# A list schedule that counts GpSimd's late begin after VectorE, with other durations and a first part of six feature blocks

## The chip, the core and the metric

The kernel runs on one NeuronCore of a Trainium2 chip. Its engines work side by side, each on its own queue of instructions: TensorE (PE in the profile, with PEld for its weight loads), VectorE (DVE), ScalarE (ACT), GpSimd (POOL), and SyncE (SP), which here starts the DMA transfers. The metric is the time of one execution on the device in microseconds; less is better.

## The reference

Banded attention over four batches, eight heads, 768 positions and a head size of 64, and behind it a feed-forward layer over the 3072 tokens (width 512, inner width 2048) whose activation is `h * cos(h)`:

```python
scores = scale * np.matmul(q, k.transpose(0, 1, 3, 2))
keep = is_global | is_local          # 8 global columns, a band of 96 behind each row
scores = np.where(keep, scores + bias, -1000000000.0)
a = np.exp(scores - np.max(scores, axis=-1, keepdims=True))
out = np.matmul(a / (np.sum(a, axis=-1, keepdims=True) + 1e-09), v)
x = out.transpose(0, 2, 1, 3).reshape(B * S, H * D)
h = x @ w_in                         # 3072 x 512 by 512 x 2048
result = (h * np.cos(h)) @ w_out     # by 2048 x 512
```

## The kernel before

The 3072 tokens are cut into eight chunks of 384. A chunk's attention is four units of two heads each, so there are 32 units. A unit is loaded, its scores are formed on TensorE (L534 for the first eight units, L538 for the others), the band is folded and the smallest value of a row taken on VectorE (L551, L560), exponentials with their sums come from ScalarE (L585), the rows are normalised (L608, L613, on VectorE or GpSimd), turned by TensorE (L675), masked on VectorE (L683, L688), multiplied with v (L710), and the result is split into a rounded part `xh` (L260 or L262) and a rest `xl` (L731).

The feed-forward layer goes by steps. One step is one chunk and one block of 128 of the 2048 features: its first product is 12 matmuls of 384 columns (L746), then come the turns (L763), the angle (L766), the cosine (L769), the product with h (L804), the split into `gh` (L260, L262 or L264) and `gl` (L813), and the second product, 9 matmuls of 512 columns (L757), some steps later. There are 8 chunks times 16 blocks, 128 steps. In what follows, step 0 is the first one, and a step's first and second product are meant by that number.

The two weight matrices come from HBM in 16 tiles each, as 64-bit words. Each of the 32 tiles is made into two float parts by six operations: `wlow` (L384, L386), `wsign` (L391, L394), `wbias` (L400, L402), `wjoin` (L405, VectorE alone), `whigh` (L260, L262, L264) and `wrest` (L415, VectorE or GpSimd). Once made, a tile stays in SBUF. The order of the steps is the list `PHASES`: chunk 0 with its first eight feature blocks, chunk 1 with all sixteen, chunk 0 with the other eight, then chunks 2 to 7 with all. So the first steps need few weight tiles and one chunk of attention.

The order on every queue is made on the host before the kernel is built, by a list scheduler (class `Plan`). Each operation has the engines that may do it with a duration in ns for each, what it comes after, the buffers it uses and a due time. Going forward in time, each free engine takes the ready operation that is due first, where another engine would not do it for less, counted with the factors `WEIGHT`. VectorE and GpSimd share a way into SBUF; the scheduler keeps those of VectorE's operations that are marked `port` and all of GpSimd's apart, and `emit` makes a GpSimd instruction wait for the marked VectorE instruction that stands before it in the plan. Where the plan leaves TensorE a gap, `emit` fills it with matmuls on zeros (L1054), up to `FILL_TO` in the plan's time.

Of the kernel before, what the change touches and what calls it, by code (L numbers as in the profile page):

```python
# [40 lines left out]
PE, ACT, DVE, POOL, SP = "PE", "ACT", "DVE", "POOL", "SP"  # L41
# [2 lines left out]
PERIOD = 5200  # L44
LAG = 3.5
MARGIN, EACH = 3.2, 3.2
EARLY = {0: 3000, 1: 6000}
WEIGHT = {PE: 1, ACT: 0.5, DVE: 1.2, POOL: 0.8}

PHASES = [(0, 0, 8), (1, 0, 16), (0, 8, 16)]  # L50

PIECES = {-1: [(0, 128), (128, 384)]}
NT, NST, NPV, NX, NV, NRAW, NQK, NRR, NG = 5, 5, 3, 2, 3, 3, 2, 3, 2
# [4 lines left out]

HOMES = 7

FILL_TO, FILL_REST, FILL_EACH, FILL_FIRST, FILL_COLD = 45000, 150, 250, 10, 7000


class Slot:


    def __init__(self, cls, make):
        self.cls, self.make = cls, make
        self.users = 0
        self.at = None  # L70
        self._tile = None
# [19 lines left out]
class Plan:  # L91
# [6 lines left out]
    TABLE = 1300  # L98
    SWITCH = 200

    def __init__(self, places, free):
        self.ops = []
        self.places = {c: list(v) for c, v in places.items()}
        self.busy = {}
        self.free = dict(free)
        self.port = 0
        self.mode = None

    def op(self, engines, emit, after=(), uses=(), due=None, table=None, extra=0, port=False, mode=None):
# [20 lines left out]
    def run(self):  # L130

        self.dues()
        for i, o in enumerate(self.ops):
            o.key = (o.due - min(o.engines.values()), i)
        ready = {e: [] for e in self.free}
        coming = []
        for o in self.ops:
            if o.left == 0:
                for e in o.engines:
                    ready[e].append(o)  # L140
        table = "exp"
        out = []
        dma = 0
        t = 0
        inf = 10**12
        todo = len(self.ops)
        import heapq

        heap = sorted(set(self.free.values()))
        while todo:  # L150
            assert heap, [(o.engines, o.key) for e in ready for o in ready[e]][:20]
            t = heapq.heappop(heap)
            while heap and heap[0] == t:
                heapq.heappop(heap)
            again = True
            while again:
                again = False
                for e, f in self.free.items():
                    if f > t:
                        continue  # L160
                    best = None
                    held = self.port > t
                    holds = lambda o, x: x == POOL or (x == DVE and o.port)
                    for o in ready[e]:
                        if o.ready > t or (best is not None and o.key >= best.key):
                            continue
                        if held and holds(o, e):
                            continue
                        if len(o.engines) > 1:
                            wait = lambda x: max(t, self.free[x], self.port if holds(o, x) else 0) - t  # L170
                            cost = lambda x: wait(x) + o.engines[x] * WEIGHT[x]
                            if any(cost(x) < cost(e) for x in o.engines if x != e):
                                continue
                        taken, ok = set(), True
                        for u in o.uses:
                            if u.at is None:
                                p = next(
                                    (p for p in self.places[u.cls] if self.busy.get(p, 0) <= t and p not in taken),
                                    None,
                                )  # L180
                                if p is None:
                                    ok = False
                                    break
                                taken.add(p)
                        if ok:
                            best = o
                    if best is None:
                        continue
                    o = best
                    if e == ACT and o.table and table and o.table != table:  # L190
                        same = [x for x in ready[e] if x.table == table and x.ready <= t]
                        if table == "exp" and same:
                            o = min(same, key=lambda x: x.key)
                    for u in o.uses:
                        if u.at is None:
                            u.at, u.begin = self.place(u, t), t
                            self.busy[u.at] = inf
                    for x in o.engines:
                        ready[x].remove(o)
                    d = o.engines[e]  # L200
                    if e == ACT and o.table and o.table != table:
                        d += self.TABLE
                        table = o.table
                    if e == PE:
                        if o.mode != self.mode:
                            d += self.SWITCH
                        self.mode = o.mode
                    o.start, o.engine = t, e
                    end = t + d
                    if holds(o, e):  # L210
                        self.port = end
                    self.free[e] = end
                    heapq.heappush(heap, end)
                    if e == SP:
                        dma = max(end + 300, dma) + o.extra

                        self.free[SP] = max(end, dma - DEPTH)
                        heapq.heappush(heap, self.free[SP])
                        end = dma + 1400
                    out.append(o)  # L220
                    todo -= 1
                    for u in o.uses:
                        u.users -= 1
                        u.end = max(getattr(u, "end", 0), end + self.WAIT[e])
                        if u.users == 0:
                            self.busy[u.at] = u.end
                            heapq.heappush(heap, u.end)
                    for n in o.then:
                        n.left -= 1
                        n.ready = max(n.ready, end + (self.WAIT[e] if list(n.engines) != [e] else 0))  # L230
                        if n.left == 0:
                            for x in n.engines:
                                ready[x].append(n)
                            heapq.heappush(heap, max(t, n.ready))
                    again = True
        self.length = max(self.free.values())
        return out


class Net:  # L240
# [123 lines left out]
    def plan_weights(self, f):  # L364


        nc, p = self.nc, self.plan
# [3 lines left out]
        for kind, src, out in (("wi", cols, self.wi), ("wo", rows, self.wo)):  # L371
# [45 lines left out]
                )  # L417

            o = p.op({SP: 470}, dma, extra=1460)
            o = p.op({ACT: 580, DVE: 500, POOL: 700}, wlow, [o], port=True)  # L420
            o = p.op({DVE: 650, POOL: 1310}, wsign, [o], port=True)
            o = p.op({ACT: 580, DVE: 345, POOL: 640}, wbias, [o], port=True)
            o = p.op({DVE: 600}, wjoin, [o], [wu], port=True)
            o = p.op({ACT: 525, DVE: 335, POOL: 595}, whigh, [o], [wu], port=True)
# [49 lines left out]
    def plan_unit(self, L, pr):  # L474
# [4 lines left out]
        nc, p, D = self.nc, self.plan, self.D  # L479
        u = dict(L, pr=pr)  # L480
        n, first = u["n"], u["first"]
# [6 lines left out]
        if exact:  # L488
# [13 lines left out]
            o = p.op({SP: 470}, load, [], [raw], extra=1422 * (QK - k0) // 1000)  # L502
# [7 lines left out]
        st = u["st"] = Slot("st", lambda i: self.work.tile([R, 6 * CT], F32, name="st", tag=i))  # L510
# [8 lines left out]
        ttr = []  # L519
        for js, h in [(js, h) for js in (((0, 1),) if exact else ((0,), (1,))) for h in range(0, CT, 2)]:  # L520
# [25 lines left out]
            for j, ps in pss.items():  # L546
# [6 lines left out]
                o = p.op({DVE: 70 + 98 * (2 - i0)}, fold, [so], [ps])  # L553
# [21 lines left out]
        def worst(e):  # L575
            nc.vector.tensor_tensor(self.worst[:R], self.worst[:R], st.tile[:, :n2], op=ALU.max)

        self.chain("worst", p.op({DVE: 80}, worst, [o for _, o in ttr], [st], due=self.xdue(n, pr), port=True))
        exps = []
        for (t, j), o in ttr:  # L580

# [13 lines left out]
        def rec(e):  # L595
            nc.vector.reciprocal(st.tile[:, 2 * n2 :], st.tile[:, n2 : 2 * n2])

        o = p.op({DVE: 85}, add, exps, [st], port=True)
        o = p.op({DVE: 120}, rec, [o], [st], port=True)
        u["norm"] = []  # L600
        for h in range(0, CT, 2):
# [169 lines left out]
    def plan_step(self, s, n, f, a, b):  # L771

        nc, p = self.nc, self.plan
        due = s * PERIOD
        x = self.x[n]
# [19 lines left out]
        for c0, c1 in pieces:  # L795
            w = c1 - c0
            cs = slice(c0, c1)
            r, h = lambda cs=cs: rr.tile[:, cs], lambda cs=cs: ph.tile[:, cs]
            act, dve, pool = 50 + w * 427 // 512, 70 + w * 535 // 512, 100 + w * 1125 // 512
            o = p.op({ACT: act}, lambda e, r=r, h=h: self.turns(e, r(), h()), [done], [ph, rr])  # L800
            o = p.op({DVE: dve}, lambda e, r=r, h=h: self.angle(e, r(), h()), [o], [ph, rr])
            o = p.op({ACT: act + 135}, lambda e, r=r: self.cosine(e, r()), [o], [rr], table="sin")
# [320 lines left out]
```

## Time and profile before

| what | value |
|---|---|
| median of 3 runs | 706.49 us (705.99 to 707.34) |
| the profiled execution | 704.92 us, its span 703.2 us |
| TensorE busy | 681.4 us (97% of the span) |
| VectorE, ScalarE, GpSimd busy | 506.0, 450.2, 140.1 us |
| granted clock over the span | 0.990 |

A share of the whole span says little here, since the kernel has two stages. In the first some 80 us all engines are at work on weights and on the attention of the first two chunks; after it TensorE hardly ever stands still. The profile is therefore read by stretches of time.

### The profile page before, as it was taken

How to read it: one execution, taken by the hardware profiler on the slowest of the kernel's cores; microseconds unless marked ns; L12 is line 12 of the kernel's file. 1: busy time of each engine (PE TensorE's matmuls, PEld its weight loads, DVE VectorE, ACT ScalarE, POOL GpSimd, SP SyncE). 2: the span in 40 equal slices, each digit the busy share in tenths (PEclk: the TensorE clock that was granted, in tenths of full speed). 3: DMA queues.
4: the chain of work that ended last, by engine and by line, in shares of the span. 5: the costliest groups of instructions: out<-in, count | busy, mean ns of one | idle time of the engine just before them, and what ended most of it. 6: DMA issues, size and time to landing. Idle time of an engine off the chain costs nothing. (4 is left out here: it accounts for less than half of the span.)

```text
span 703.2 us, 12932 instructions
## 1 busy us (share of the span) xinstructions
PE 681.4 (97%) x4448; PEld 595.5 (85%) x4448; DVE 506.0 (72%) x1531; ACT 450.2 (64%) x1129; POOL 140.1 (20%) x180
## 2 busy tenths in 40 slices
PE   8988899999999999999999999999999999999995
PEld 5666799888898888989888898888889888998994
DVE  7998988997847778478776877568784877733442
ACT  6899996776736666467666666476673666634342
POOL 4565665433002121010000121011000112000000
PEclk8999999999999999999999999999999999999998
DMA  9998600013223322032320422212122300001001
GB/s 296 322 305 255 194 22 25 24 46 84 86 67 98 78 60 59 1 104 66 69 68 1 113 62 59 59 57 71 43 68 69 113 27 2 1 1 46 0 1 50
DMA packets 32603, 55.74 MB, mean 79 GB/s; under 512 B 3472, under 2 KB 18192, under 8 KB 32528
## 3 DMA queue, kind: packets, MB, share of 16 engines
q1 hardware_dynamic: 32528, 54.82, 27.1%
q8 instruction: 37, 0.61, 0.4%
q14 instruction: 38, 0.31, 0.1%
HBM read 48.52 MB, written 6.29 MB: 78 GB/s over the span
## 5 line engine op out<-in xcount | busy, mean ns | idle before, releaser
L746 PE MATMUL bank<-xh,w 128*128 128x384 f32 x1024 | 296.7, 343 | 0.6 <-DVE rr L804 0.6
L757 PE MATMUL bank<-w,gh 128*128 128x512 f32 x768 | 245.5, 401 | 0.0
L746 PEld LDWEIGHTS bank<-xh,w 128*128 128x128 f32 x1024 | 188.7, 188 | 8.0 <-DVE rr L804 1.5
L746 PE MATMUL bank<-xl,w 128*128 128x384 f32 x512 | 173.3, 339 | 0.2 <-DVE xl L731 0.2
L757 PEld LDWEIGHTS bank<-w,gh 128*128 128x128 f32 x768 | 138.3, 188 | 22.1 <-issue 0.5
L757 PE MATMUL bank<-w,gl 128*128 128x512 f32 x384 | 151.5, 395 | 0.0
L763 ACT ACTIVATE rr<-bank 128x384 int32<-128x384 f32 x129 | 62.0, 482 | 130.8 <-PE bank L746 128.9
L766 DVE SCALAR_TENSOR_TENSOR rr<-rr,bank 128x384 f32<-128x384 int32 x129 | 69.9, 542 | 103.3 <-ACT rr L763 102.9
L769 ACT ACTIVATE rr<-rr,half_pi 128x384 f32<-128x384 f32 x129 | 78.6, 613 | 40.2 <-DVE rr L766 38.6
L746 PEld LDWEIGHTS bank<-xl,w 128*128 128x128 f32 x512 | 96.7, 189 | 4.3 <-DVE xl L731 0.4
L804 DVE TENSOR_TENSOR rr<-bank,rr 128x384 f32<-128x384 f32 x129 | 70.6, 551 | 37.7 <-ACT rr L769 37.4
L585 ACT ACTIVATE tt<-tt,st 96x104 f32<-96x104 f32 (+1 forms) x256 | 94.3, 370 | 3.9 <-DVE st L560 3.3
L757 PEld LDWEIGHTS bank<-w,gl 128*128 128x128 f32 x384 | 72.1, 188 | 17.3
L813 DVE TENSOR_TENSOR gl<-rr,gh 128x384 fp32r<-128x384 f32 (+1 forms) x114 | 67.9, 595 | 10.2 <-ACT gh L260 7.4
L264 POOL TENSOR_SCALAR ks<-raw 128x408 fp32r<-128x408 f32 (+1 forms) x34 | 19.4, 570 | 273.7 <-PE bank L538 204.7
L260 ACT CAST gh<-rr 128x384 fp32r<-128x384 f32 (+1 forms) x97 | 49.2, 508 | 27.4 <-DVE rr L804 18.8
L560 DVE CUSTOM_DVE_ANT_0 tt<-bank,dd 96x104 f32<-96x104 f32 (+1 forms) x256 | 55.8, 257 | 2.9
L710 PEld LDWEIGHTS bank<-pv,v 104*64 104x64 f32 (+1 forms) x960 | 42.6, 140 | 12.2 <-issue 7.7
L710 PE MATMUL bank<-pv,v 104*64 104x96 f32 (+1 forms) x960 | 49.1, 254 | 1.2 <-ACT pv L260 1.2
L538 PEld LDWEIGHTS bank<-ks,qs 128*96 128x96 f32 x384 | 45.8, 162 | 4.7 <-issue 0.3
L585 ACT ACTIVATION_READ_ACCUMULATOR tt<-tt,st 96x1 f32 x256 | 48.1, 188 | 0.0
L538 PE MATMUL bank<-ks,qs 128*96 128x200 f32 (+1 forms) x384 | 47.9, 254 | 0.0
(95 smaller groups left out, 705.3 us busy)
## 6 DMA issues: line engine op xcount, KB each, us to landing
raw<-in_qk_dram SPq DMA_DIRECT2D x48, 224.0 KB
raw<-in_qk_dram SPq DMA_DIRECT2D x48, 198.0 KB
raw<-in_w_in_dram SPq DMA_DIRECT2D x16, 512.0 KB
raw<-in_w_out_dram SPq DMA_DIRECT2D x16, 512.0 KB
out_dram<-oo SPq DMA_DIRECT2D x24, 256.0 KB
v<-in_v_dram SPq DMA_DIRECT2D x16, 240.0 KB
v<-in_v_dram SPq DMA_DIRECT2D x16, 192.0 KB
raw<-in_qk_dram SPq DMA_DIRECT2D x4, 448.0 KB
```

Of the source, the lines that this page charges most:

```text
L260: self.nc.scalar.copy(out, x)
L538: nc.tensor.matmul(out, qs[:, m, q0], ks[:, k : k + w], start=m == 0, stop=m == 1)
L560: nc.vector.tensor_tensor_reduce(tt[t // 2].tile[:, t % 2, j, :w], ps.tile[:R, i * WIN : i * WIN + w], self.dd[:, v, :w], op0=ALU.add, op1 ...
L585: nc.scalar.activation(x, x, AF.Exp, bias=st.tile[:, c : c + 1], scale=-1.0, accum_out=st.tile[:, n2 + c : n2 + c + 1])
L710: nc.tensor.matmul(px.tile[j * D : (j + 1) * D, t * R : (t + 1) * R], vs.tile[:k, t + c, hs][:, j * D : (j + 1) * D], pv[:k, c, o : o + R] ...
L746: self.nc.tensor.matmul(ph[:, :CW], self.wi[f][:, w, kk * P : (kk + 1) * P], xx[:, kk, :], start=kk == 0 and m == 0, stop=kk == self.NK - ...
L757: self.nc.tensor.matmul(po, gg[:, ts], self.wo[f][:, w, :], start=start and m == 0, stop=stop and m == 2)
L763: self.nc.scalar.activation(r.bitcast(I32), ph, AF.Copy, scale=1.0 / TWO_PI, bias=0.25)
L766: self.nc.vector.scalar_tensor_tensor(r, r.bitcast(I32), -TWO_PI, ph, op0=ALU.mult, op1=ALU.add)
L769: self.nc.scalar.activation(r, r, AF.Sin, bias=self.half_pi)
L804: {DVE: dve}, lambda e, r=r, h=h: nc.vector.tensor_tensor(r(), h(), r(), op=ALU.mult), [o], [ph, rr]
L813: self.eng(e).tensor_tensor(g[1][:, cs], r(), g[0].bitcast(F32)[:, cs], op=ALU.subtract)
```

## The change

The scheduler gets a time `HAND` of 170 ns: GpSimd begins nothing until so long after a marked VectorE operation has ended, and this waiting is counted where an operation's engine is chosen. Some durations are raised: two of GpSimd's weight operations and its `gl` by 40, 40 and 20 ns, and two small ones on VectorE. GpSimd's factor in the choice falls from 0.8 to 0.6, chunk 0's due times are spread by 2000 rather than 3000, chunk 0's first part has six feature blocks rather than eight, and gaps are filled until 100,000 rather than 45,000 ns of the plan. No operation is added to or taken from the computation; all that differs is the order on the queues, which engine does what, and how many filler matmuls there are.

```diff
-EARLY = {0: 3000, 1: 6000}
-WEIGHT = {PE: 1, ACT: 0.5, DVE: 1.2, POOL: 0.8}
-PHASES = [(0, 0, 8), (1, 0, 16), (0, 8, 16)]
+EARLY = {0: 2000, 1: 6000}
+WEIGHT = {PE: 1, ACT: 0.5, DVE: 1.2, POOL: 0.6}
+PHASES = [(0, 0, 6), (1, 0, 16), (0, 6, 16)]
-FILL_TO, FILL_REST, FILL_EACH, FILL_FIRST, FILL_COLD = 45000, 150, 250, 10, 7000
+FILL_TO, FILL_REST, FILL_EACH, FILL_FIRST, FILL_COLD = 100000, 150, 250, 10, 7000
...
+    HAND = 170
...
-                        if held and holds(o, e):
+                        if held and holds(o, e) or e == POOL and self.hand > t:
                             continue
                         if len(o.engines) > 1:
-                            wait = lambda x: max(t, self.free[x], self.port if holds(o, x) else 0) - t
+                            turn = lambda x: (self.hand if x == POOL else 0, self.port if holds(o, x) else 0)
+                            wait = lambda x: max(t, self.free[x], *turn(x)) - t
...
                     if holds(o, e):
                         self.port = end
+                        if e == DVE:
+                            self.hand = end + self.HAND
+                            heapq.heappush(heap, self.hand)
...
-            o = p.op({ACT: 580, DVE: 500, POOL: 700}, wlow, [o], port=True)
-            o = p.op({DVE: 650, POOL: 1310}, wsign, [o], port=True)
+            o = p.op({ACT: 580, DVE: 500, POOL: 740}, wlow, [o], port=True)
+            o = p.op({DVE: 650, POOL: 1350}, wsign, [o], port=True)
...
-        self.chain("worst", p.op({DVE: 80}, worst, [o for _, o in ttr], [st], due=self.xdue(n, pr), port=True))
+        self.chain("worst", p.op({DVE: 100}, worst, [o for _, o in ttr], [st], due=self.xdue(n, pr), port=True))
...
-        o = p.op({DVE: 85}, add, exps, [st], port=True)
+        o = p.op({DVE: 195}, add, exps, [st], port=True)
...
-            act, dve, pool = 50 + w * 427 // 512, 70 + w * 535 // 512, 100 + w * 1125 // 512
+            act, dve, pool = 50 + w * 427 // 512, 70 + w * 535 // 512, 120 + w * 1125 // 512
```

Lines of the kernel after stand up to six further down than before (`wjoin` is L405 before and L411 after). Two places show what moves. The first is VectorE's queue before the normalisation of the eighth unit, whose turning closes the first stage on TensorE; `tt` is a tile of exponentials, `wu` a joined weight tile, `st` the row sums. Before:

```order
L576 TENSOR_TENSOR worst_115<-worst_115,st_806 96x8
L391 TENSOR_SCALAR raw_131<-raw_131 128x512
L415 TENSOR_TENSOR w_1108<-wu_1099,w_1108 128x512
L731 TENSOR_TENSOR xl_853<-bank_1080,xh_852 128x384
L593 TENSOR_SCALAR st_1040<-st_1040 96x8
L596 RECIPROCAL st_1040<-st_1040 96x8
L405 SCALAR_TENSOR_TENSOR wu_1132<-raw_129 128x512
L613 TENSOR_TENSOR tt_1039<-tt_1039,st_1040 96x416
```

After:

```order
L810 TENSOR_TENSOR rr_988<-bank_942,rr_988 128x384
L582 TENSOR_TENSOR worst_115<-worst_115,st_1009 96x8
L411 SCALAR_TENSOR_TENSOR wu_1101<-raw_127 128x512
L819 TENSOR_TENSOR gl_1078<-rr_932,gh_1077 128x384
L411 SCALAR_TENSOR_TENSOR wu_1113<-raw_129 128x512
L599 TENSOR_SCALAR st_1009<-st_1009 96x8
L602 RECIPROCAL st_1009<-st_1009 96x8
L397 TENSOR_SCALAR raw_134<-raw_134 128x512
L619 TENSOR_TENSOR tt_1008<-tt_1008,st_1009 96x416
L619 TENSOR_TENSOR tt_1080<-tt_1080,st_1009 96x416
```

Before, only one half of the unit is normalised here (L613) and the other half is GpSimd's; after, both halves stand here (L619), and the `wrest` that stood in this stretch (L415) has gone.

The second place is GpSimd's queue in the middle of that stage. Before:

```order
L386 TENSOR_SCALAR raw_127<-raw_127 128x512
L402 TENSOR_SCALAR raw_125<-raw_125 128x512
L813 TENSOR_TENSOR gl_785<-rr_703,gh_784 128x384
L394 TENSOR_SCALAR raw_132<-raw_132 128x512
L386 TENSOR_SCALAR raw_134<-raw_134 128x512
L394 TENSOR_SCALAR raw_127<-raw_127 128x512
L394 TENSOR_SCALAR raw_134<-raw_134 128x512
L386 TENSOR_SCALAR raw_136<-raw_136 128x512
L386 TENSOR_SCALAR raw_138<-raw_138 128x512
L415 TENSOR_TENSOR w_970<-wu_959,w_970 128x512
L415 TENSOR_TENSOR w_998<-wu_975,w_998 128x512
L386 TENSOR_SCALAR raw_142<-raw_142 128x512
```

After:

```order
L619 TENSOR_TENSOR tt_621<-tt_621,st_622 96x416
L619 TENSOR_TENSOR tt_729<-tt_729,st_622 96x416
L270 TENSOR_SCALAR gh_812<-rr_679 128x384
L421 TENSOR_TENSOR w_789<-wu_774,w_789 128x512
L819 TENSOR_TENSOR gl_813<-rr_679,gh_812 128x384
L270 TENSOR_SCALAR gh_854<-rr_699 128x384
L400 TENSOR_SCALAR raw_127<-raw_127 128x512
L819 TENSOR_TENSOR gl_855<-rr_699,gh_854 128x384
L408 TENSOR_SCALAR raw_127<-raw_127 128x512
L400 TENSOR_SCALAR raw_129<-raw_129 128x512
L400 TENSOR_SCALAR raw_131<-raw_131 128x512
L421 TENSOR_TENSOR w_978<-wu_964,w_978 128x512
```

Before, the rows are mostly `wlow` and `wsign` (L386, L394); after, `wlow` is gone from here, and two normalisations (L619), three `wrest` (L421), two `gh` (L270) and two `gl` (L819) stand between the `wsign` (L400). Counted over GpSimd's queue up to where the eighth unit is turned, `wlow` goes from 12 to 3, `wrest` from 3 to 7, whole normalisations from 0 to 4 and `gh` from 0 to 3.

## Rows read from the trace of the kernel before

**Rows 1.** Busy time by stretches: us, then each engine's busy us (instructions), clock, DMA share, GB/s.

```profile
20.00:40.00 20.00, 18.34 (x169) 12.50 (x170) 19.93 (x77) 18.48 (x54) 10.86 (x11) 1.00 0.97 283
40.00:60.00 20.00, 16.55 (x115) 13.08 (x115) 18.00 (x60) 18.59 (x53) 11.27 (x12) 0.91 0.86 284
60.00:80.00 20.00, 16.39 (x141) 13.16 (x141) 19.30 (x63) 19.88 (x50) 12.47 (x13) 1.00 1.02 306
100.00:120.00 20.00, 20.00 (x102) 18.15 (x101) 15.01 (x25) 14.47 (x29) 11.61 (x10) 1.00 0.15 41
7.64:78.59 70.95, 59.96 (x501) 45.24 (x497) 66.76 (x265) 64.95 (x197) 39.40 (x42) 0.93 0.97 306
```

**Rows 2.** Timeline of TensorE: start us, us, instructions, [idle before <- releaser].

```profile
48.99 0.51 PE L675 MATMUL bank<-ident,tt 96*104 96x96 f32 x4 [2.13 <-DVE pv L688]
...
52.63 2.12 PE L710 MATMUL bank<-pv,v 104*64 104x96 f32 x32
...
78.59 0.51 PE L675 MATMUL bank<-ident,tt 96*104 96x96 f32 x4 [2.07 <-DVE tt L613]
...
93.79 0.64 PE L757 MATMUL bank<-w,gh 128*128 128x512 f32 x2
```

**Rows 3.** Pieces of the chain that ended last: start us, us, what.

```profile
443.60 1.48 PE bank L710 x32
...
452.31 2.12 PE bank L746 x12
454.43 2.11 PE bank L757 x9
```

**Rows 4.** VectorE by line, 10 to 84 us: busy us, mean ns | idle before, releaser.

```profile
L405 DVE SCALAR_TENSOR_TENSOR wu<-raw 128x512 uint32<-128x512 uint32 x14 | 9.4, 676 | 0.0
L415 DVE TENSOR_TENSOR w<-wu,w 128x512 fp32r<-128x512 f32 x10 | 7.8, 784 | 0.1
L613 DVE TENSOR_TENSOR tt<-tt,st 96x416 f32<-96x416 f32 x11 | 6.9, 649 | 0.0
...
L813 DVE TENSOR_TENSOR gl<-rr,gh 128x384 fp32r<-128x384 f32 x3 | 2.2, 749 | 0.0
...
L391 DVE TENSOR_SCALAR raw<-raw 128x512 uint16<-128x512 uint16 x2 | 1.5, 734 | 0.0
```

**Rows 5.** ScalarE by line, 10 to 84 us.

```profile
L384 ACT ACTIVATE raw<-raw 128x512 int32<-128x512 uint32 x13 | 8.5, 677 | 0.0
L400 ACT ACTIVATE raw<-raw 128x512 f32<-128x512 f32 x10 | 6.8, 683 | 1.3 <-POOL raw L394 1.3
L260 ACT CAST w<-wu 128x512 fp32r<-128x512 f32 x11 | 6.7, 612 | 0.2 <-DVE worst L576 0.2
L769 ACT ACT_TABLE_LOAD x5 | 6.4, 1283 | 0.1
L585 ACT ACT_TABLE_LOAD x4 | 5.1, 1283 | 0.1
...
L260 ACT CAST xh<-bank 128x384 fp32r<-128x384 f32 x7 | 3.3, 467 | 2.1 <-PE bank L710 2.1
```

**Rows 6.** Timeline of ScalarE.

```profile
54.79 0.48 ACT L260 CAST xh<-bank 128x384 fp32r<-128x384 f32 x1 [1.07 <-PE bank L710]
...
87.83 1.14 ACT L260 CAST w<-wu 128x512 fp32r<-128x512 f32 x2
```

**Rows 7.** TensorE's filler matmuls, 0 to 90 us, by line.

```profile
L1054 PE MATMUL idle<-zeros 128*128 128x512 bf16 x30 | 9.4, 464 | 1.1 <-DVE zeros L270 1.1
```

**Rows 8.** GpSimd by line, 10 to 84 us.

```profile
L394 POOL TENSOR_SCALAR raw<-raw 128x512 bf16<-128x512 bf16 x14 | 18.8, 1355 | 15.2 <-DVE wu L405 7.3 <-DVE w L415 4.1 <-DVE st L596 3.0
L386 POOL TENSOR_SCALAR raw<-raw 128x512 int32<-128x512 uint32 x12 | 9.3, 772 | 6.3 <-DVE tt L613 4.5 <-DVE wu L405 1.1
L415 POOL TENSOR_TENSOR w<-wu,w 128x512 fp32r<-128x512 f32 x4 | 5.2, 1288 | 4.9 <-DVE raw L391 2.1 <-ACT rr L763 1.7 <-ACT tt L585 1.1
...
L613 POOL TENSOR_TENSOR tt<-tt,st 96x416 f32<-96x416 f32 x1 | 0.9, 877 | 1.5 <-DVE tt L613 1.5
```

More of the change, by code (lines that the diff above doesn't have):

```diff
@@ L105, in __init__ @@
         self.free = dict(free)
-        self.port = 0
+        self.port = self.hand = 0
         self.mode = None
```

## The prediction

> **What bounds the kernel now.** I read the busy times by stretches first [rows 1]. TensorE is busy for 20.00 of the 20 us from 100 to 120, but for 16.55 and 16.39 of 20 from 40 to 60 and 60 to 80, and filler matmuls are counted as busy there. In those early stretches VectorE is busy for 18.00 to 19.93 of 20 and ScalarE for 18.48 to 19.88. So the kernel has a first stage that VectorE and ScalarE set, and behind it TensorE works without a gap on a load that the change leaves alone: the same matmuls, only in another order. What the change is worth is what it makes of the time that TensorE loses in the first stage.
>
> Where that stage ends is seen in TensorE's timeline [rows 2]: at 78.59 the eighth unit is turned, after 2.07 us of waiting for a normalisation on VectorE. From there on no long gap follows. A microsecond by which this point comes earlier, with the same TensorE work done by then, is a microsecond of the whole.
>
> I need TensorE's own pace to say what "the same work" is. In the chain that ended last [rows 3], a first product takes 2.12 us for 12 matmuls, 0.177 each, a second product 2.11 for 9, 0.234 each, and a unit's product with v 1.48 for 32.
>
> **The change on VectorE.** I counted in both orders what has to be done on each queue before TensorE can turn the eighth unit: everything that stands ahead of the last instruction it needs. On VectorE, after against before: `wjoin` 11 for 13, `wrest` 2 for 9, whole normalisations 7 for 11, one `wsign` and one `gl` fewer. By the means of [rows 4] that is 2 x 0.676 + 7 x 0.784 + 4 x 0.649 + 0.734 + 0.749 = 10.9 us less. One product of the cosine and one small operation more cost at most 0.65 each, the length of a normalisation: I take 9.6 less. Two weight casts fewer and two casts of `xh` more I set equal; all of them are shorter than a normalisation.
>
> TensorE by then has done nine matmuls more of the first products and nine fewer of the second: 9 x 0.177 - 9 x 0.234 = 0.5 us that it owes. If VectorE alone set the point, it would come 9.6 - 0.5 = 9.1 us earlier. That is the upper bound of the gain.
>
> **What is late next: ScalarE.** `wlow`, which GpSimd gives up, goes to ScalarE, and ScalarE had little room. For every first and second product I compared the work that ScalarE must have done with TensorE's own; the difference is largest, after the change, at the second product of step 6. There, after against before, ScalarE has ahead of it six `wlow` and two `wbias` more, one weight cast, two `xh` casts and one scaling of queries fewer, two `gh` fewer for two copies of an output part more, and two table loads fewer, one of each kind. By [rows 5] that is 6 x 0.677 + 2 x 0.683 - 0.612 - 2 x 0.467 - 0.68 - 2 x 1.283 = 0.6 us more; the scaling is counted as long as a `wbias`, and `gh` against part is set at nothing, as both are moves of the same kind, with 0.5 either way kept for the range.
>
> Before, the last ScalarE instruction that this product needs is the first of two weight casts that begin at 87.83 [rows 6]; at 0.612 it ends at 88.44, and TensorE reaches the product at 93.79 [rows 2], 5.35 us later. This is how far TensorE can move up before ScalarE stops it. After the change TensorE stands at that place with 12 matmuls of a first product less behind it, 12 x 0.177 = 2.1 us that it still has to do. So 5.35 - 0.6 - 2.1 = 2.6 us are to be had there if ScalarE idles as much as before.
>
> **The fillers and the clock.** ScalarE idled for 1.07 us before the cast at 54.79 [rows 6], waiting for a product with v that took 2.12 us [rows 2] instead of 1.48 [rows 3]. The granted clock is 0.91 over 40 to 60 and 1.00 over the stretches around it [rows 1], so part of that stretch ran at 1.2 and not 2.4 GHz; TensorE had stood still for 2.13 us before 48.99 [rows 2]. These two rows are the fifth unit's. The new program has 50 fillers before the eighth unit's turning for 30, and 13 of them stand around the fifth unit's turning and product, so I take this wait as gone: 1.0 us, between 0 (the clock falls elsewhere) and 1.3 (twice the 0.64 lost in that product).
>
> The 30 fillers of before take 9.4 us together [rows 7], 0.31 each. The 20 additional ones cost nothing where they lie in gaps; TensorE was idle for 1.66 + 3.45 + 3.61 = 8.7 us from 20 to 80 [rows 1], and each run of them stands ahead of an operation that waits for VectorE or GpSimd. Without that cover they cost 20 x 0.31 = 6.2 us.
>
> **GpSimd.** Up to the eighth unit its queue has nine `wlow` fewer, one `wsign`, four `wrest` and four whole normalisations more, and three others more on balance. By [rows 8]: -9 x 0.772 + 1.355 + 4 x 1.288 + 4 x 0.877 + 3 x 0.772 = +5.4 us. Between 7.64 and 78.59 it was busy for 39.40 of 70.95 us [rows 1], so there is room, 31 us of it. Most of the idle time before its rows is ended by a VectorE instruction [rows 8], and VectorE's shared instructions shrink by the 10.9 us above.
>
> Here a rule of the Trainium skill weighs in. SBUF — State Buffer, section "SBUF: two separate sides", says that the port pair which VectorE and GpSimd share is an exclusive lock, held for a whole instruction. By it the sum over both engines would set the stage: 10.9 less and 5.4 more. The rows agree in so far as a `wrest` on VectorE took 0.784 us by mean; but the kernel itself makes GpSimd wait for VectorE, so the trace does not separate the lock from that order.
>
> **The sum.** 2.6 us at ScalarE's tight place and 1.0 for its wait that goes: 3.6 us less. After that stage 25% of VectorE's time and 28% of ScalarE's are free from 100 to 120 [rows 1], so the weight tiles put off, two of 13, are made there without TensorE waiting; I take nothing for it, and keep 1 us either way for other short waits. The profiled execution took 704.92 us, 1.72 around a span of 703.2, and lies 1.6 under the median of the runs. I take the difference off the median: 706.49 - 3.6 = 702.9.
>
> **Rivals.**
>
> *ScalarE is not the limit (larger gain).* It idles less because what it waited for, VectorE's work, comes earlier. Then the limit is VectorE at 9.1, or VectorE and GpSimd together with 10.9 - 5.4 - 0.5 = 5.0; I take 7.0: 699.5. By the rule of SBUF — State Buffer in the Trainium skill it would be the 5.0. For it speaks that VectorE is the engine TensorE waits for at 78.59. Against it, that ScalarE is busy for 19.88 of 20 us from 60 to 80.
>
> *GpSimd becomes the bound (slower).* Its place is the second product of step 2. Everything GpSimd must have done by then comes to 39.40 less two `wlow` that it did beyond need, plus 5.4, so 43.3 us. TensorE has 18 matmuls of the second products less behind it there than at 78.59, 4.2 us, so GpSimd would have to be ready at 74.4, 66.8 us after 7.64: a busy share of 65%. Below that the change loses. From 40 to 80 the share was 23.74 of 40, or 59% [rows 1]; at this share it takes 73.4 us, 6.6 too many: 713.1. For it: long `wrest`, normalisations and `gl` now stand in one queue in a fixed order. Against it: its idle time was VectorE's doing, and that shrinks.
>
> *The gain is hidden (no change).* The second products of the first steps are reordered, and `gh` and `gl` now follow each other on GpSimd; a 1 us wait behind the fillers at two or three places, or 3 us of uncovered fillers, takes up the 3.6: 706.
>
> *The new cost of a hand-over doesn't match the chip.* Then the plan is no nearer to the trace than before, and only the counts act; they are what I have summed, so this alone changes no price and has no chance of its own.
>
> **Chances.** The forecast, a gain of 1.4 to 5.5 us, 0.46, its own range 701 to 705. The larger gain 0.18, no change 0.18, slower 0.18. About 0.2%, 1.4 us, is what a measurement of this kernel can tell from no change. So faster 0.64, same 0.18, slower 0.18. The range goes from 698.5, which leaves out the extreme of the larger gain, to 708, which leaves out the worse half of the slower case.
>
> **What would show it.** The turning of the eighth unit should begin near 71 to 75 us instead of 78.59, and TensorE should be without gaps from there. ScalarE should be busy for over 95% from 40 to 75, with `wlow` on it, and VectorE for less than before. The second product of step 6 should begin near 92.3 (93.79 - 3.6 + 2.1) or earlier. The granted clock from 40 to 60 should be 1.00. I am wrong if TensorE's waits before L681 or L763 end with GpSimd instructions (the slower rival), if the eighth unit comes earlier by 3 us or more and the time stays (lost later, to weight tiles put off), or if TensorE's work by that point differs from the count.

## The result

The changed kernel takes 697.41 us (median of 4, 696.88 to 698.08), the kernel before 706.39 beside it (median of 4, 705.99 to 707.34): a ratio of 0.9873, 95% interval 0.9861 to 0.9886, or 9.0 us less. Run again beside other kernels it took 697.46 against 705.49, ratio 0.9886 (0.9869 to 0.9902). The forecast of 702.9 had the sign and less than half of the size, and its range began at 698.5. The two profiled executions lie closer together than the medians: spans of 703.2 and 696.4 us, 6.8 apart.

The busy times of the changed kernel by stretches answer to [rows 1] (us, then PE, PEld, DVE, ACT and POOL busy, granted clock, DMA share, GB/s):

```profile
0.00:20.00 20.00, 16.57 (x124) 10.03 (x124) 14.52 (x88) 13.89 (x58) 10.62 (x43) 0.91 0.88 285
20.00:40.00 20.00, 19.84 (x179) 13.96 (x180) 19.18 (x80) 18.75 (x65) 13.77 (x14) 1.00 0.99 330
40.00:60.00 20.00, 19.54 (x166) 14.84 (x164) 18.52 (x63) 19.68 (x49) 14.19 (x14) 1.00 0.94 310
60.00:80.00 20.00, 18.54 (x147) 15.00 (x146) 18.61 (x54) 19.88 (x44) 11.02 (x10) 1.00 0.93 279
100.00:120.00 20.00, 20.00 (x101) 18.11 (x100) 15.50 (x26) 12.21 (x24) 10.49 (x10) 1.00 0.15 41
```

TensorE's idle time from 20 to 80 us falls from 8.7 to 2.1, and the stretch from 40 to 60 runs at full clock. GpSimd is busier from 20 to 60 (28.0 us for 22.1). Over 15 to 100 us, first the kernel before (with its first 20 us, for the clock) and then the changed one, it is ScalarE that does more, 3.5 us, while VectorE does 1.5 less and GpSimd the same:

```profile
0.00:20.00 20.00, 16.56 (x118) 10.94 (x118) 14.53 (x86) 12.54 (x50) 10.86 (x41) 0.83 0.92 309
...
15.00:100.00 85.00, 76.23 (x586) 60.52 (x583) 79.11 (x251) 77.86 (x203) 50.35 (x49) 0.95 0.75 235
```

```profile
15.00:100.00 85.00, 82.78 (x643) 64.97 (x642) 77.64 (x247) 81.40 (x210) 50.57 (x48) 0.99 0.73 237
```

TensorE's timeline after, for [rows 2]: the fifth unit's product with v, the eighth unit's turning, the second product of step 6.

```profile
43.08 1.55 PE L716 MATMUL bank<-pv,v 104*64 104x96 f32 x32
...
72.23 1.01 PE L681 MATMUL bank<-ident,tt 96*104 96x96 f32 x8
...
86.97 0.64 PE L763 MATMUL bank<-w,gh 128*128 128x512 f32 x2
```

The product takes 1.55 us for 2.12, the turning stands 6.4 us earlier and waits for nothing (the first row has no bracket), the second product 6.8 earlier. What TensorE waited for from 15 to 100 us (us in total, times, longest), before and after:

```profile
PE bank L675 <- DVE tt L613: 3.4, 3, 2.1
PE bank L675 <- DVE pv L688: 3.3, 2, 2.1
PE bank L746 <- DVE rr L804: 0.6, 2, 0.4
```

```profile
PEld bank L681 <- POOL tt L619: 1.3, 2, 0.7
PE bank L681 <- DVE pv L694: 1.2, 1, 1.2
...
PE bank L752 <- DVE rr L810: 0.3, 1, 0.3
PE bank L681 <- DVE xl L737: 0.2, 1, 0.2
```

As idle time the waits for normalisations (L613) are gone; behind fillers, weight loads (PEld) still wait 1.3 us for two of GpSimd's normalisations (L619). VectorE's and GpSimd's work from 7.64 us to the turning, for [rows 4, 8], is what the count said: 11 `wjoin` (L411), 2 `wrest` (L421) and 8 normalisations (L619, one of them needed later) on VectorE; on GpSimd `wrest` and normalisations for `wlow` (L392).

```profile
L411 DVE SCALAR_TENSOR_TENSOR wu<-raw 128x512 uint32<-128x512 uint32 x11 | 8.2, 745 | 0.0
...
L619 DVE TENSOR_TENSOR tt<-tt,st 96x416 f32<-96x416 f32 x8 | 4.4, 583 | 0.0
L421 DVE TENSOR_TENSOR w<-wu,w 128x512 fp32r<-128x512 f32 x2 | 1.4, 677 | 0.0
```

```profile
L400 POOL TENSOR_SCALAR raw<-raw 128x512 bf16<-128x512 bf16 x13 | 17.3, 1360 | 0.3 <-ACT tt L591 0.2
L421 POOL TENSOR_TENSOR w<-wu,w 128x512 fp32r<-128x512 f32 x7 | 9.0, 1288 | 8.8 <-DVE wu L411 3.2 <-ACT w L266 2.9 <-DVE w L421 2.7
L619 POOL TENSOR_TENSOR tt<-tt,st 96x416 f32<-96x416 f32 x4 | 3.5, 880 | 1.4 <-DVE wu L411 1.4
...
L392 POOL TENSOR_SCALAR raw<-raw 128x512 int32<-128x512 uint32 x3 | 2.0, 658 | 0.2
```

GpSimd's idle time before `wsign` (L400 after, L394 before) falls from 15.2 us to 0.3, but most of it stands before other operations now, 8.8 us before `wrest` (L421): from 10 to 84 us GpSimd idles for 31.6 us before and 27.7 after.

### The profile page after: what moved, and what is told of

It is laid out like the page before. It is cut to its first block, busy times and chain, and to the rows that moved or that the text cites. A ratio compares the mean times of both kernels' runs of the same rounds, so it can differ in the third digit from the quotient of the medians.

```text
span 696.4 us, 12970 instructions
## 1 busy us (share of the span) xinstructions
PE 681.7 (98%) x4469; PEld 595.7 (86%) x4469; DVE 485.8 (70%) x1482; ACT 460.3 (66%) x1145; POOL 167.6 (24%) x215
## 4 chain that ended last, share of the span: by engine, by line
PE 86%; ACT 6%; DVE 5%; issue 1%; DMA 1%; POOL 1%; SPq 0%; ACTq 0%; DVEq 0%; POOLq 0%
PE bank L752 36%; PE bank L763 35%; PE bank L716 5%; PE bank L544 5%; PE bank L681 3%; ACT tt L591 1%; ACT L591 1%; PE bank L540 1%; PE idle L1060 1%; ACT L775 1%; POOL tt L614 1%; DVE tt L566 1%; DVE bank L557 1%; ACT rr L775 1%; DVE ks L649 1%
## 5 line engine op out<-in xcount | busy, mean ns | idle before, releaser
L752 PEld LDWEIGHTS bank<-xh,w 128*128 128x128 f32 x1024 | 188.2, 188 | 10.2 <-DVE rr L810 3.1
L819 DVE TENSOR_TENSOR gl<-rr,gh 128x384 fp32r<-128x384 f32 (+1 forms) x105 | 59.6, 568 | 15.4 <-ACT gh L266 6.8
L270 POOL TENSOR_SCALAR ks<-raw 128x408 fp32r<-128x408 f32 (+1 forms) x30 | 17.2, 574 | 193.7 <-PE bank L544 191.3
L716 PEld LDWEIGHTS bank<-pv,v 104*64 104x64 f32 (+1 forms) x960 | 41.1, 136 | 11.0 <-issue 6.0
L819 POOL TENSOR_TENSOR gl<-rr,gh 128x384 fp32r<-128x384 f32 (+1 forms) x24 | 24.0, 1000 | 104.0 <-ACT gh L266 80.7
```

The costliest lines, as they stand in the source:

```text
L716: nc.tensor.matmul(px.tile[j * D : (j + 1) * D, t * R : (t + 1) * R], vs.tile[:k, t + c, hs][:, j * D : (j + 1) * D], pv[:k, c, o : o + R] ...
L752: self.nc.tensor.matmul(ph[:, :CW], self.wi[f][:, w, kk * P : (kk + 1) * P], xx[:, kk, :], start=kk == 0 and m == 0, stop=kk == self.NK - ...
L819: self.eng(e).tensor_tensor(g[1][:, cs], r(), g[0].bitcast(F32)[:, cs], op=ALU.subtract)
```

## The experiments

Times are medians; a difference is against the changed kernel (697.4) or against the kernel before in the same group of runs (705.4 to 706.1).

**Work added to one engine.** Six idle instructions of 128 x 512 were put on one engine, in the fixed order where they do nothing but take time: 0.60 us each on ScalarE (3.6 in all), 0.66 on VectorE (4.0).

```diff
...
# with the exponentials (pad_act) ...
+                if n == 1 and pr > 0 and j == 0 and t % 2 == 0:
+                    nc.scalar.copy(self.pad, self.ident.rearrange("p (o w) -> p o w", o=1).broadcast_to([P, 4, P]))
# ... or ahead of the reciprocals (pad_dve)
+            for _ in range(2 if n == 1 and pr > 0 else 0):
+                nc.vector.tensor_reduce(
+                    self.pad, self.ident.rearrange("p (o w) -> p o w", o=1).broadcast_to([P, 4, P]),
+                    axis=mybir.AxisListType.X, op=ALU.max,
+                )
```

> The changed kernel with six idle copies of 512 columns (about 0.57 us each, 3.4 in all) on ScalarE, two with the exponentials of each of the sixth to eighth units. Theory S (ScalarE is the next limit, its room at the second product of step 6 is used up): 2.4 to 3.4 us slower. Theory V (VectorE, with GpSimd, still sets the stage; ScalarE had idled and idles less): slower by less than 1 us.

> The changed kernel with six idle reductions of 512 columns (about 0.55 us each, 3.3 in all) on VectorE, two ahead of the reciprocals of each of the sixth to eighth units. Theory S: 0 to 1.3 us slower, as VectorE has room of its own. Theory V: 2.3 to 3.3 us slower.

> The kernel before with the same six copies on ScalarE. By the 5.35 us of room that I read at the second product of step 6, both theories say under 0.8 us slower; over 2 us slower would mean that this room was never there.

> The kernel before with the same six reductions on VectorE. Both theories have VectorE set the eighth unit's turning here: 2.3 to 3.3 us slower. Under 1 us would mean that VectorE never was the limit.

In the changed kernel ScalarE's copies cost 1.9 us (699.35) and VectorE's reductions 4.4 (701.84); in the kernel before 3.2 (708.65) and 3.3 (708.75). On the changed kernel neither theory holds: S has ScalarE too high and VectorE far too low, V has both too low. On the kernel before both are right on VectorE and fail on ScalarE, where there was no room either. Of the time added, from 1.9 of 3.6 us (ScalarE, changed) to 4.4 of 4.0 (VectorE, changed) reaches TensorE. I take it that this is because both engines hand work to each other in a fixed order; the traces were not followed from wait to wait.

**Work added to ScalarE behind the turning**, where my step saw the room of 5.35 us:

```diff
-    def turns(self, e, r, ph):
+    def turns(self, e, r, ph, s=-1):
+        for _ in range(2 if s in (5, 6, 7) else 0):
+            self.nc.scalar.copy(self.pad, self.ident.rearrange("p (o w) -> p o w", o=1).broadcast_to([P, 4, P]))
...
```

> The changed kernel with six idle copies on ScalarE (0.60 us each, 3.6 in all, as measured in the first pads), two ahead of each first use of the phases of steps 5 to 7: between the last ScalarE work that the eighth unit's turning needs and the second product of step 6. By my step (room of 5.35 us before, less what the change used, some 0.8 left): 2 to 3.6 us slower than the changed kernel. Theory V: under 1 us slower.

> The kernel before with the same six copies at the same steps. By my step (5.35 us of room): under 0.7 us slower than before. If ScalarE's work counts wherever it stands: 2 to 3.6 us slower.

It costs 3.9 us in the changed kernel (701.36) and 3.3 in the kernel before (708.81), where my step had under 0.7: the room of 5.35 us was not there. The trace of the latter shows where: not at a second product, but at a first product (PE L747), which waits for the multiplication with the cosine (DVE L807) of the step two earlier.

```profile
89.84 0.44 PE L747 MATMUL bank<-xh,w 128*128 128x384 f32 x1 [1.14 <-DVE rr L807]
```

```profile
84.11 0.54 DVE L807 TENSOR_TENSOR rr<-bank,rr 128x384 f32<-128x384 f32 x1
89.23 0.56 DVE L807 TENSOR_TENSOR rr<-bank,rr 128x384 f32<-128x384 f32 x1
```

The second multiplication ends at 89.79 and the product begins at 89.84: the multiplication reads what the first product of its step has written from a PSUM bank, and the program uses two such banks in turn. I had followed what a product reads, not who must free the bank that it writes. The same pairs, of steps 7 and 8, in the kernel before:

```profile
84.54 0.44 PE L746 MATMUL bank<-xh,w 128*128 128x384 f32 x1
...
87.45 0.34 PE L746 MATMUL bank<-xh,w 128*128 128x384 f32 x1
```

```profile
82.68 0.54 DVE L804 TENSOR_TENSOR rr<-bank,rr 128x384 f32<-128x384 f32 x1
85.91 0.56 DVE L804 TENSOR_TENSOR rr<-bank,rr 128x384 f32<-128x384 f32 x1
```

The room was 84.54 - 83.22 = 1.3 us and 87.45 - 86.47 = 1.0. At the five steps ahead of these there was none: the first products of steps 2 to 6 of the kernel before begin 0.05 to 0.06 us after the multiplication two steps earlier ends. At two of them, steps 2 and 5, the trace has TensorE idle for it; at the others a turning (L675) stands just ahead, and the trace does not say which of the two they waited for.

```profile
39.29 0.54 DVE L804 TENSOR_TENSOR rr<-bank,rr 128x384 f32<-128x384 f32 x1
68.39 0.55 DVE L804 TENSOR_TENSOR rr<-bank,rr 128x384 f32<-128x384 f32 x1
```

```profile
39.89 0.44 PE L746 MATMUL bank<-xh,w 128*128 128x384 f32 x1 [0.26 <-DVE rr L804]
68.99 0.45 PE L746 MATMUL bank<-xh,w 128*128 128x384 f32 x1 [0.37 <-DVE rr L804]
```

In the changed kernel the room of step 8 is used up: 84.75 against 84.14 + 0.55.

```profile
84.75 0.44 PE L752 MATMUL bank<-xh,w 128*128 128x384 f32 x1
```

```profile
84.14 0.55 DVE L810 TENSOR_TENSOR rr<-bank,rr 128x384 f32<-128x384 f32 x1
```

**Parts of the change alone**, on the kernel before, and one undone:

```diff
# o_weight, on the kernel before
-WEIGHT = {PE: 1, ACT: 0.5, DVE: 1.2, POOL: 0.8}
+WEIGHT = {PE: 1, ACT: 0.5, DVE: 1.2, POOL: 0.6}
# o_handdur, on the kernel before: the scheduler's lines and all durations of the change
+    HAND = 170
# o_phases, on the kernel before
-PHASES = [(0, 0, 8), (1, 0, 16), (0, 8, 16)]
+PHASES = [(0, 0, 6), (1, 0, 16), (0, 6, 16)]
# u_weight, on the changed kernel
-WEIGHT = {PE: 1, ACT: 0.5, DVE: 1.2, POOL: 0.6}
+WEIGHT = {PE: 1, ACT: 0.5, DVE: 1.2, POOL: 0.8}
```

> The kernel before with GpSimd's weight alone (0.6 for 0.8). Counted up to the second product of step 6, its order has 7.5 us less on VectorE and 9.4 more on GpSimd than before, 0.4 more on ScalarE. Theory V (VectorE's count sets the stage): 5 to 9 us faster than before. Theory S (ScalarE's room ends the gain): 2.6 to 5 faster. Theory L (VectorE and GpSimd can't work beside each other, their sum counts): 1 to 2 slower.

> The kernel before with the 170 ns of hand-over and the new durations alone. To the second product of step 6 its order has 4.9 us more on VectorE, 5.2 less on GpSimd, ScalarE as before. Theories V and S: 3 to 5 us slower than before. Theory L: within 1 us of before.

> The kernel before with six feature blocks in the first part for eight, alone. To the second product of step 6 VectorE has 0.5 us less, GpSimd 1.8 less, ScalarE 0.3 less. Theories V and S: within 1 us of before. Theory L: 2.3 us faster.

> The changed kernel with GpSimd's weight put back to 0.8. To the second product of step 6, against before, VectorE has 2.2 us less, ScalarE 3.2 less, GpSimd 5.7 less; to the eighth unit's turning VectorE has 0.8 more. Theory V: within 2 us of before, so 6 to 9 slower than the changed kernel. Theory S: as V or, by ScalarE's count, 3 faster than before. Theory L: 8 faster than before, as fast as the changed kernel.

The weight alone gives 5.7 us (700.35; ratio 0.9910, 0.9894 to 0.9927), and without it the changed kernel is 12 us slower (709.37), slower than before. Hand-over and durations alone cost 4.2 (710.23), the six blocks alone 1.9 (707.93). The parts don't add up: -5.7 + 4.2 + 1.9 = +0.4, and together they give 8 to 9. Two parts are not in this sum, since the early time and the wider `FILL_TO` were not run alone on the kernel before. Theory L falls on all four. Theory S misses the time of o_weight (5.7 for at most 5), o_phases and u_weight. Theory V has the signs of three; it missed the size of u_weight, and o_phases by its median, though the interval there (0.4 to 3.2 us) reaches within 1.

**Other parts undone, and the fillers.**

```diff
# u_hand; u_handdur has the old durations as well
-    HAND = 170
+    HAND = 0
# u_early
-EARLY = {0: 2000, 1: 6000}
+EARLY = {0: 3000, 1: 6000}
# u_phases
-PHASES = [(0, 0, 6), (1, 0, 16), (0, 6, 16)]
+PHASES = [(0, 0, 8), (1, 0, 16), (0, 8, 16)]
# u_fill20
-FILL_TO, FILL_REST, FILL_EACH, FILL_FIRST, FILL_COLD = 100000, 150, 250, 10, 7000
+FILL_TO, FILL_REST, FILL_EACH, FILL_FIRST, FILL_COLD = 20000, 150, 250, 10, 7000
```

> The changed kernel without the 170 ns of hand-over and with the old durations. To the second product of step 6 its order has, against the changed kernel and less TensorE's own work, 6.9 us less on VectorE, 5.6 less on ScalarE, GpSimd equal; to the eighth unit's turning 3.0 less on VectorE. Theory V (counts): 3 to 7 us faster than the changed kernel. Theory P (an order is worth what its plan knows of the chip; without the hand-over it lets VectorE and GpSimd wait for each other): 2 to 6 slower.

> The changed kernel without the fillers behind 20 us of its plan, the order of all other work unchanged. Theory C (the fillers keep TensorE's clock): the granted clock falls below 1.00 in one or more stretches between 20 and 100 us and the kernel is 2 to 5 us slower. Theory N (they only fill gaps; my term of 1.0 us for the fifth unit's wait was the most they give): 0 to 1.3 us slower, or faster by under 1.

> The changed kernel once more, beside the next three. Every theory: 697.4 us within 0.7, some 8 to 9 us below the kernel before. It shows how far its executions lie apart.

> The changed kernel with the early time of the first part put back to 3000. New theory B: the first product of a step waits for VectorE's multiplication with the cosine two steps earlier, which frees its bank. At the worst of these places (steps 5 to 12) VectorE's count, less TensorE's own work, is 3.8 us higher here than in the changed kernel (34.8 in the kernel before, 28.1 in the changed one, 31.9 here), ScalarE's equal. B: 2 to 4 us slower than the changed kernel. Theory S at my old place (second product of step 6; ScalarE 3.4 lower there): not slower.

> The changed kernel with eight feature blocks in its first part. At the places of theory B VectorE has 1.3 us more and ScalarE 1.7 more than in the changed kernel: 1 to 2.5 us slower. Theory S at my old place (ScalarE 3.1 lower): not slower.

Without both hand-over and durations the time is the same (698.05): theories V and P are both wrong there. With the early time put back it is 4.6 us slower (702.02), with eight blocks 1.5 (698.99): theory B has the sign of both, the size of the second, and 2 to 4 for the first. The trace of u_early has the wait that B speaks of, at step 4, ahead of the steps that I had counted:

```profile
61.95 0.44 PE L752 MATMUL bank<-xh,w 128*128 128x384 f32 x1 [2.12 <-DVE rr L810]
```

Without the fillers behind 20 us it is 3.9 us slower (701.36), theory C. The clock falls (busy times by stretches):

```profile
20.00:40.00 20.00, 16.63 (x144) 12.97 (x143) 16.47 (x76) 16.74 (x60) 13.36 (x13) 0.76 0.94 316
40.00:60.00 20.00, 17.06 (x148) 14.68 (x147) 17.00 (x60) 17.85 (x45) 11.58 (x13) 0.91 0.82 286
```

At 0.76 about half of these 20 us ran at 1.2 and not 2.4 GHz, and TensorE stood still for 3.4 of them; with the fillers the clock is 1.00 there.

**Further than the change.** Counting the work ahead of each multiplication that frees a bank, I looked for orders with still less on VectorE and ScalarE.

```diff
# u_hd_w5, on u_handdur
-WEIGHT = {PE: 1, ACT: 0.5, DVE: 1.2, POOL: 0.6}
+WEIGHT = {PE: 1, ACT: 0.5, DVE: 1.2, POOL: 0.5}
# u_hd_p4, on u_handdur
-PHASES = [(0, 0, 6), (1, 0, 16), (0, 6, 16)]
+PHASES = [(0, 0, 4), (1, 0, 16), (0, 4, 16)]
```

> GpSimd's weight lowered to 0.5, without the 170 ns and the new durations. At the places of theory B VectorE has 5.2 us less than in the changed kernel, ScalarE 1.9 less, while GpSimd gets the low halves of the gated products as well. B: 2 to 5 us faster than the changed kernel. Theory G (GpSimd, slower at each of these, is now late itself): 1 to 6 us slower.

> The changed kernel with the 170 ns of hand-over set to 0, all else kept. At the places of theory B VectorE has 1.9 us less than in the changed kernel and ScalarE 1.7 less; GpSimd has 488 instructions for 407. B: 1 to 2 us faster than the changed kernel (some 696). Theory P (the hand-over has to be in the plan): 2 to 6 slower.

> The changed kernel without hand-over and new durations and with four feature blocks in its first part: of the versions counted, the one with least on ScalarE (5.1 us less than the changed kernel at the places of theory B) and 1.8 less on VectorE; GpSimd has 491 instructions. B: 1 to 2.5 us faster than the changed kernel (some 695.5), and so faster than both kernels.

All three are slower than the changed kernel: u_hd_w5 by 19.7 us (717.13), u_hand by 6.2 (703.67), u_hd_p4 by 5.2 (702.65). Theory B is wrong on each of them. Theory P has the sign of u_hand, at 6.2 just outside its 2 to 6, and theory G the sign of u_hd_w5, which lost over three times its 6 us. B describes the first 100 us at most. From 15 to 100 us TensorE idles for only 1.9, 1.8 and 1.7 us in them, 2.2 in the changed kernel; what they lose comes later. u_hd_w5 from 100 to 200 us, its busy times and TensorE's longest waits:

```profile
100.00:200.00 100.00, 88.12 (x514) 75.64 (x514) 56.51 (x164) 74.55 (x172) 77.32 (x75) 0.95 0.20 55
```

```profile
PE bank L763 <- POOL w L421: 7.4, 4, 2.7
PE bank L763 <- ACT w L266: 2.1, 2, 1.4
```

Here GpSimd is the bound: busy for 77 of 100 us, with weights that come late for the second products. In u_hand, TensorE idles for 6.2 us from 100 to 680 (2.0 in the changed kernel), of which 3.6 are ended by GpSimd and 1.5 by ScalarE:

```profile
100.00:680.00 580.00, 573.80 (x3674) 508.24 (x3674) 371.94 (x1084) 360.26 (x875) 162.95 (x198) 1.00 0.19 53
```

```profile
PE bank L681 <- POOL tt L614: 1.8, 6, 0.4
...
PE bank L763 <- POOL w L421: 1.1, 1, 1.1
PE bank L681 <- POOL tt L619: 0.7, 3, 0.4
```

So the hand-over in the plan is worth 6.2 us with the new durations, and the pair of them nothing. Between the profiles, 5.5 us apart, 4.2 of it are waits behind 100 us. Why the order without both, which gives GpSimd as much, avoids these waits is open. In u_hd_p4 one wait for GpSimd stands out, and from 128.75 to 135.5 us, around and behind it, the granted clock was 0.50:

```profile
129.28 1.05 PE L681 MATMUL bank<-ident,tt 96*96 96x96 f32 x4 [2.60 <-POOL tt L614]
```

## Where the time went

TensorE's time of each profiled execution can be written as a ledger, in us: idle to 100 us; fillers; what the clock took (stretches of 10 us, each times 1 less its granted clock); idle from 100 us to 25 before the end; and the rest of the span.

| kernel | span | idle to 100 | fillers | clock | idle later | rest |
|---|---|---|---|---|---|---|
| before | 703.2 | 12.2 | 9.5 | 5.1 | 2.5 | 674.0 |
| changed | 696.4 | 5.6 | 15.8 | 1.7 | 2.0 | 671.3 |
| changed, again | 695.0 | 6.9 | 14.4 | 0.0 | 2.0 | 671.7 |
| u_fill20 | 701.4 | 11.3 | 6.9 | 10.3 | 2.0 | 670.9 |
| o_weight | 698.7 | 6.4 | 14.4 | 1.7 | 1.8 | 674.3 |
| o_handdur | 709.9 | 13.4 | 11.3 | 10.2 | 2.6 | 672.4 |
| u_hand | 701.9 | 4.9 | 14.7 | 1.7 | 6.2 | 674.4 |
| u_hd_w5 | 715.8 | 5.1 | 14.6 | 1.7 | 18.5 with its clock | 675.9 |

The rest stays within 671 to 676 while spans differ by 21, so the four columns hold most of what separates these kernels. Between before and changed they say: idle time to 100 us -6.6, fillers +6.3, clock -3.4, later idle time -0.5, rest -2.7, together -6.9 for a measured -6.8. Idle time has become filler time, of nearly the same length; what is saved is mostly slow matmuls. The filler row for [rows 7] shows the one half:

```profile
L1060 PE MATMUL idle<-zeros 128*128 128x512 bf16 x51 | 15.8, 444 | 1.1 <-DVE zeros L276 1.1
```

The two executions of the changed kernel show the other: one had the clock at 0.91 in its first 20 us, the other at 1.00, and their spans differ by 1.4 us.

The columns are rough: the clock's takes a slow row's idle time for lost time too, and fillers that overlap are counted twice. The slow stretches themselves, two before (12.90 and 50.43) and one after, stand in the records at 0.50, which is 1.2 GHz:

```profile
12.90:19.70 6.80, 6.36 (x52) 5.20 (x52) 5.24 (x30) 4.42 (x18) 4.68 (x6) 0.50 1.03 407
50.43:53.83 3.40, 3.40 (x24) 2.96 (x24) 3.36 (x16) 3.06 (x14) 1.77 (x3) 0.50 0.89 284
```

```profile
13.30:16.70 3.40, 3.40 (x17) 1.75 (x19) 2.74 (x17) 2.97 (x16) 2.54 (x3) 0.50 1.03 408
```

Half of the 9.8 us of matmuls in the first two was lost, 4.9; of the 3.4 in the last some 1.4 are fillers, so 1.0 was lost. With overlaps counted once, the time up to the second product of step 6, 93.79 before and 86.97 after, differs by: idle time -6.6, fillers +5.9, slow clock -3.9, the 12 matmuls of a first product not yet done -2.1, all else -0.1, together -6.8. Behind that product both kernels take 609.4 us, though the changed one still has those 12 matmuls to do: 2.1 us are gained there, 0.5 of them in idle time. What makes up the other 1.6 I could not find.

The columns depend on each other. u_fill20 has the order of the changed kernel, and its slow clock takes 8.6 us more; its span is only 5.0 longer, since idle time and fillers come to 18.2 for 21.4: a slower TensorE waits less. The wider `FILL_TO` is not needed for the clock: o_weight has 45,000 still, 45 fillers and the clock column of the changed kernel.

## Why the prediction was wrong

**VectorE's count, and the turning at 71 to 75**: right. The counts of the order stand in the trace, and the turning came 6.4 us earlier, 5.9 less what TensorE owed; of the upper bound of 9.1 two thirds. The time set for the second product of step 6, "near 92.3 (93.79 - 3.6 + 2.1)", has the 2.1 with the wrong sign: with 12 matmuls less behind it the product comes earlier by them, so my sum meant 93.79 - 3.6 - 2.1 = 88.1. It came at 86.97.

**"What is late next: ScalarE", 5.35 - 0.6 - 2.1 = 2.6**: the step that failed. The place was wrong, since the products' banks tie first products to VectorE's multiplication and so to ScalarE two steps earlier; the room there was not 5.35 but 1.3 and 1.0 at steps 7 and 8, as pad_late_before shows, and none at steps 2 to 6. And the condition "if ScalarE idles as much as before" did not hold: it was busy for 3.5 us more of the same 85. The first error makes the term too large, the second too small, so it is luck that the sum came out near at this place: TensorE gained 6.8 - 2.1 = 4.7 us there for my 2.6 + 1.0 = 3.6. It was not made up as I had it: the shorter waiting that I gave 2.6 came to 0.7 (idle time -6.6, fillers +5.9), and the clock to 3.9.

**The clock, 1.0 between 0 and 1.3**: mis-sized. I charged it with one wait of ScalarE and not with TensorE's own matmuls. The slow stretches cost 3.9 us less, 2.2 of it in the first 20 us, where I had not looked; taking the fillers behind 20 us out of the changed kernel costs 3.9. That the additional fillers cost nothing was right: idle time and fillers to 100 us come to 21.7 before and 21.4 after.

**"After that stage I take nothing"**: too low by the 2.1 us behind step 6's second product, of which only the 0.5 in idle time is explained.

**The spread of executions** adds the remaining 2.2 to 4.7 + 2.1: the gain is 6.8 between the profiles and 9.0 between the medians, as the profiled execution of before lies 1.5 us under the median of its runs and that of the changed kernel 0.7 above.

**GpSimd becomes the bound**: not at this weight, but one step further (u_hd_w5) the kernel lost 19.7 us, behind 100 us and not at the second product of step 2. **ScalarE is not the limit**, priced at 7.0, was the rival that came nearest, and ScalarE did idle less, as it says. Its limit by an exclusive lock, the rule of SBUF — State Buffer ("SBUF: two separate sides") in the Trainium skill, does not show as a bound here: theory L, the sum of both engines' work, had the wrong sign for o_weight and u_weight. That doesn't test the lock itself, since the kernel keeps these engines apart by its own order.

## What to carry to other kernels

Ask of a matmul not only who makes what it reads but who frees the bank it writes: room read from the first alone was 5.35 us here where the second left 1.0 or none. Where two engines hand work to each other in a fixed order, idle time on one is not room; put some idle work on it and measure. Price a slow clock by the matmuls that run in it, over the whole stretch, and not by one wait behind them.

## What was not expected of the hardware

Filling TensorE's idle time with idle matmuls was worth 3.9 us although they take nearly as long as the gaps. And with GpSimd busy for 77 of 100 us (u_hd_w5) TensorE stood still for 11.9 us of that stretch, most of it waiting for GpSimd, while at 28 of 40 (20 to 60 us of the changed kernel) no idle time of TensorE of 0.2 us or more ended with GpSimd; weight loads behind fillers did wait for it.
